# K's split projection: two accumulating matmuls of 128 columns in place of one of 256 and an addition

## The chip, the cores and the metric

The kernel runs on one core of a Trainium2 chip. Its engines, by the names of the profile, are PE (TensorE: matmuls; PEld are its weight loads), DVE (VectorE), ACT (ScalarE), POOL (GpSimd) and SP (SyncE, which issues nearly all DMAs). The metric is the device time of one execution in microseconds (us), lower is better.

## The reference

Linear attention with a feature map, followed by a block that mixes tokens and channels. What matters here is the first half; `phi(k)` begins with the product that the change rewrites.

```python
# q, k, v: (8, 8, 576, 64) float32; w_phi: (64, 128)
def phi(x):
    proj = np.einsum('bhsd,df->bhsf', x, w_phi)
    proj = proj - np.max(np.abs(proj), axis=-1, keepdims=True)
    return np.concatenate([np.exp(proj), np.exp(-proj)], axis=-1)
q_p, k_p = (phi(q), phi(k))
kv = np.einsum('bhsf,bhsd->bhfd', k_p, v)
z = np.sum(k_p, axis=2)
num = np.einsum('bhsf,bhfd->bhsd', q_p, kv)
den = np.einsum('bhsf,bhf->bhs', q_p, z)[..., None] + 1e-06
x = num / den            # heads joined: (8, 576, 512)
# then, per batch, with U (576 x 32), V (32 x 576), w_ch1 (512 x 2048), w_ch2 (2048 x 512):
h = x.transpose(0, 2, 1) @ U @ V
u = x + h.transpose(0, 2, 1)
out = u + np.maximum(u @ w_ch1, 0.0) @ w_ch2
```

## The kernel before

**Pairs of heads.** Attention works on pairs of heads of one batch, 8 x 4 = 32 pairs (`Pair`). Of the 576 tokens of a head, 512 are the main part, in four tiles of 128; the last 64 are the tail. For each pair the steps are: projecting K's tail and head 0 (`s_project_k0`), head 1 and Q's tail (`s_project_k1`), Q (`s_project_q0`, and the second half in `s_kv0_q1`), the sums over tokens of features times V (`kv_main`, line 448), and Q's features times these sums (`out_main`, line 487). The steps of one pair are interleaved with the output steps of the pair before.

**Split values.** Float32 products on TensorE are made here from parts in the type fp32r: a value is its rounded part (hi) plus what is left (lo). Batches 0 and 1 project K with plain float32 matmuls (line 389). Batches 2 to 7, with 24 pairs and thus 48 calls of `project_k_split`, use the parts. There `T[0]` holds K turned around, 128 partitions with the 64 hi parts and the 64 lo parts of a column one above the other, as [128, 2, 512]: the second index is the half of the tokens, the last is head and token within the half. `w_hl` is [128, 2, 128]: w_phi's hi part and its lo part, each written twice, one above the other. A matmul of a block of 128 tokens of `T[0]` (the weights) with `w_hl[:, n, :]` therefore gives (k_hi + k_lo) times one part of w_phi; the sum over n = 0, 1 is the projection.

**The call before the change** (lines 396 to 410). For each s of 0, 1, one PSUM bank `pk` takes two matmuls of 256 columns (line 404): each multiplies a block of tokens with both parts at once, and leaves the two products side by side. ACT copies the half that belongs to w_lo into the not yet used first half of the feature tile `kp` (line 407), and DVE adds the half that belongs to w_hi, into the second half of `kp` (line 408). Then `k_features` follows: the largest absolute value of each token (DVE, line 353), its subtraction (DVE, line 355), and the two exponentials (ACT, lines 358 and 359). In batches 0 and 1 `k_features` reads the PSUM bank directly.

**The tails** are the other place where parts of w_phi accumulate: `project_k_tail` (lines 378 and 379) and `project_q_tail` (lines 416 and 417) issue two matmuls of 128 columns of fp32r into the same columns of a bank.

**PSUM.** Eight banks in three groups: "at" with 3 banks (all tiles of attention: transposed tails `tT`, `pkt`, `pk`, `pqt`, `pq`, `kv_ps`, `xpt`, `xp`, and some of the token mixing), "ph" with 1 (hidden units of the mixer) and "o" with 4 (the mixer's outputs). A tile of a group waits until the tile that had its bank before is no longer read.

**The channel mixer** is most of TensorE's work: `hidden` (line 631) and `add` (line 652), each three matmuls of 512 columns for one product, one chunk of 128 hidden units after the other. `Pace` deals out the chunks of a batch among the attention steps of the next one, so TensorE finds matmuls while a step of attention waits for ACT and DVE.

**Order.** The program is built with `schedule_with_timeline_sim=True`: the framework's planner lays down each engine's order from its own estimated costs when the kernel is built; on the chip each engine runs its instructions in that order, and TensorE takes its matmuls in order.

Of the kernel before, what the change touches and what calls it, by code (L numbers as in the profile page):

```python
# [17 lines left out]
ALU = mybir.AluOpType  # L18
# [3 lines left out]
P = 128  # L22
# [3 lines left out]
def tile_kernel(  # L26
# [12 lines left out]
    nc = tc.nc  # L39
    B, H, S, D = q.shape  # L40
    F = w_phi.shape[1]
# [6 lines left out]
    NT = S // P  # L48
# [38 lines left out]
    w_hl = const.tile([P, 2, F], F32R, name="w_hl")  # L87
# [166 lines left out]
    class Pair:  # L254
# [140 lines left out]

        def project_k_split(self, g):

            kp = self.k_tile(g, NT)
            k_w = kp[:, :, F:2 * F]
            for s in range(2):  # L400
                pk = self.ps(f"pk{g}{s}_").rearrange("p (t n f) -> p t n f", t=2, n=2)
                for i in range(2):
                    cs = slice((2 * g + s) * P, (2 * g + s + 1) * P)
                    nc.tensor.matmul(  # L404
                        pk[:, i, :, :], self.T[0][:, i, cs], w_hl, start=True, stop=True)
                ts_ = slice(s, NT, 2)
                nc.scalar.copy(out=kp[:, ts_, 0:F], in_=pk[:, :, 1, :])
                nc.vector.tensor_tensor(
                    out=k_w[:, ts_, :], in0=pk[:, :, 0, :], in1=kp[:, ts_, 0:F], op=ALU.add)
            return self.k_features(g, k_w, kp)  # L410

        def project_q_tail(self):
            pq = self.ps("pqt")
# [535 lines left out]
```

## Time and profile before

| | us |
|---|---|
| median of two runs | 1218.74 (1218.65 to 1218.82) |
| the profiled execution | 1219.22 |
| its span, first to last instruction | 1217.4 |
| matmuls of line 404, x192: sum by the profile | 35.0 |
| copies of line 407 on ACT, x96 | 33.3 |
| additions of line 408 on DVE, x96 | 37.5 |
| first and last start of a matmul on line 404 | 197.0 and 977.8 |

Busy times of PE are sums over matmuls that overlap, with modelled ends, so the distance from one start to the next is what a matmul costs in a row of matmuls. Groups of instructions are written as line, engine, operation, out<-in, partitions x elements and count, then busy time in us and the mean of one in ns, then the idle time of the engine before them and what ended it. In the order of time a row gives the start, the length, the engine and the count of instructions merged into it.

### The profile page before, as it was taken

The page shows a single profiled execution, that of the slowest core. Times are in us where ns is not written, and L with a number is a line of the kernel's source. Part 1 is how long each engine was busy: PE and PEld are TensorE (multiplying, and loading weights), DVE is VectorE, ACT ScalarE, POOL GpSimd, SP SyncE. Part 2 cuts the span into 40 slices and gives each one's busy share as a digit, 9 for nine tenths or more (in the row PEclk, how much of TensorE's full clock was granted, in tenths as well). Part 3 has the DMA queues.
Part 4 walks back from the last instruction along what each step waited for, and adds up shares of the span by engine and source line. Part 5 has one row for each costly group of instructions (what it writes and reads, how often), then busy time and mean ns, then how long its engine had stood idle before and what let it go on. Part 6 is the DMA issues. An engine that isn't in the chain of part 4 may idle for free.

```text
span 1217.4 us, 18242 instructions
## 1 busy us (share of the span) xinstructions
PE 1193.5 (98%) x6669; PEld 1029.9 (85%) x6669; DVE 667.5 (55%) x1482; ACT 537.2 (44%) x1151; POOL 204.9 (17%) x154
## 2 busy tenths in 40 slices
PE   6999998999999999999999999999999999999998
PEld 5977887888888888888888888888888888888886
DVE  5667678765566556764647556765656542311211
ACT  5778787454443545344435454344444431111110
POOL 3334444211110111011111111011101110000000
PEclk8999999999999999999999999999999999999999
DMA  4686121331235123431244123521343015410201
GB/s 115 218 273 238 48 62 30 104 99 30 65 95 111 42 48 87 87 99 30 66 121 108 29 54 85 130 49 29 93 102 99 1 53 145 119 35 1 69 1 35
DMA packets 248290, 100.61 MB, mean 83 GB/s; under 512 B 215304, under 2 KB 227848, under 8 KB 248200
## 3 DMA queue, kind: packets, MB, share of 16 engines
q1 hardware_dynamic: 246928, 98.16, 30.9%
q10 hardware_dynamic: 1272, 1.28, 0.4%
q8 instruction: 53, 0.87, 0.3%
q14 instruction: 37, 0.30, 0.1%
HBM read 78.41 MB, written 20.97 MB: 82 GB/s over the span
## 4 chain that ended last, share of the span: by engine, by line
PE 88%; DVE 5%; DMA 2%; ACT 2%; SPq 1%; issue 1%; POOL 0%; DVEq 0%; ACTq 0%; POOLq 0%
PE ph L631 31%; PE o L652 30%; PE kv_ps L448 8%; PE xp L487 8%; PE pk L404 2%; PE pp L567 1%; PE kv_ps L441 1%; PE xpt L474 1%; PE pq L427 1%; PE pq L428 1%; SPq L270 1%; PE pq L432 1%; DVE w L240 1%; PE vp L585 1%; PE pk L389 1%
## 5 line engine op out<-in xcount | busy, mean ns | idle before, releaser
L631 PE MATMUL ph<-uT_hi,w 128*128 128x512 f32 x1152 | 389.3, 395 | 1.7 <-ACT uT_hi L248 1.1
L652 PE MATMUL o<-w,h_hi 128*128 128x512 f32 x1152 | 327.7, 395 | 0.7 <-ACT h_hi L636 0.7
L631 PEld LDWEIGHTS ph<-uT_hi,w 128*128 128x128 f32 x1152 | 216.3, 188 | 46.8 <-ACT uT_hi L248 1.8
L652 PEld LDWEIGHTS o<-w,h_hi 128*128 128x128 f32 x1152 | 211.1, 188 | 41.9 <-ACT h_hi L636 1.4
L631 PE MATMUL ph<-uT_lo,w 128*128 128x512 f32 x576 | 225.0, 391 | 0.3 <-DVE uT_lo L249 0.3
L636 ACT ACTIVATE h_hi<-ph 128x512 fp32r<-128x512 f32 x144 | 86.0, 597 | 278.9 <-PE ph L631 268.0
L637 DVE SCALAR_TENSOR_TENSOR h_lo<-ph,h_hi 128x512 fp32r<-128x512 f32 x144 | 98.7, 685 | 176.7 <-ACT h_hi L636 175.4
L652 PE MATMUL o<-w,h_lo 128*128 128x512 f32 x576 | 192.2, 395 | 0.0
L368 POOL PARTITION_ALL_REDUCE qp<-qp x64 | 127.0, 1984 | 296.8 <-ACT qp L367 274.8
L487 PEld LDWEIGHTS xp<-kv,qp 128*128 128x128 f32 x1024 | 122.6, 192 | 5.4 <-ACT w L239 0.8
L448 PEld LDWEIGHTS kv_ps<-vb,kp 128*128 128x128 f32 x1024 | 124.3, 192 | 2.8
L631 PEld LDWEIGHTS ph<-uT_lo,w 128*128 128x128 f32 x576 | 108.3, 188 | 21.6 <-DVE uT_lo L249 0.8
L487 PE MATMUL xp<-kv,qp 128*128 128x65 f32 x1024 | 122.9, 272 | 1.1 <-DVE x L466 0.7
L448 PE MATMUL kv_ps<-vb,kp 128*128 128x65 f32 x1024 | 123.7, 270 | 0.0
L652 PEld LDWEIGHTS o<-w,h_lo 128*128 128x128 f32 x576 | 105.2, 188 | 20.5 <-DVE h_lo L637 0.2
L358 ACT ACTIVATE kp<-kp 128x512 f32<-128x512 f32 x64 | 40.4, 632 | 125.9 <-DVE kp L355 88.7
L368 POOL PARTITION_ALL_REDUCE qp_t<-qp_t x32 | 27.3, 853 | 401.1 <-ACT qp_t L367 401.1
L324 DVE TENSOR_TENSOR T<-raw,T 64x512 fp32r<-64x512 f32 x96 | 68.2, 711 | 34.0 <-ACT T L323 31.5
L323 ACT CAST T<-raw 64x512 fp32r<-64x512 f32 x96 | 59.4, 618 | 34.7 <-PE pq L428 26.0
L320 DVE STREAM_TRANSPOSE raw<-raw 128x512 f32<-128x512 f32 x48 | 34.1, 711 | 67.8 <-DMA raw<-in_q_dram 24.8
L370 ACT ACTIVATE qp<-qp 128x512 f32<-128x512 f32 x64 | 40.4, 632 | 50.6 <-DVE qp L369 50.1
L145 POOL INT64_ADD w_ab<-w_ab x32 | 44.9, 1404 | 67.8 <-DVE w_ab L141 63.0
(125 smaller groups left out, 1324.2 us busy)
## 6 DMA issues: line engine op xcount, KB each, us to landing
words<-in_moe_w_ch_dram SPq DMA_DIRECT2D x32, 512.0 KB, 8.4
w<-kept SPq DMA_DIRECT2D x30, 512.0 KB, 4.0
vb<-in_v_dram SPq DMA_DIRECT2D x64, 128.0 KB, 2.4
u_dram<-x SPq DMA_DIRECT2D x32, 256.0 KB, 2.1
st<-u_dram SPq DMA_DIRECT2D x16, 512.0 KB, 3.8
out_dram<-st SPq DMA_DIRECT2D x32, 256.0 KB, 2.3
y<-u_dram SPq DMA_DIRECT2D x112, 64.0 KB, 2.2
raw<-in_k_dram SPq DMA_DIRECT2D x192, 32.0 KB, 1.8
```

The source lines that it names most:

```text
L145: nc.gpsimd.int64_add(a64, a64, b64)
L323: nc.scalar.copy(out=m[here, s, :], in_=x_[here])
L324: nc.vector.tensor_sub(m[there, s, :], x_[here], f32(m[here, s, :]))
L358: nc.scalar.activation(out=kp[:, :, 0:F], in_=kp[:, :, F:2 * F], func=AF.Exp)
L368: nc.gpsimd.partition_all_reduce(qp[:, 0, :], qp[:, 1, :], P, ReduceOp.absmax)
L370: nc.scalar.activation(out=qp[:, 0, :], in_=qp[:, 1, :], func=AF.Exp)
L448: nc.tensor.matmul(self.kv_v[:, f, g, :], kp[:, t, f * F:(f + 1) * F], self.vb[:, g, t, :], start=False, stop=(t == NT - 1), skip_group_ch ...
L487: nc.tensor.matmul(xv[:, c, :], qp[:, f, c * P:(c + 1) * P], self.kv[:, f, c // 2 if self.split else s, :], start=(f == 0), stop=(f == 1))
L631: nc.tensor.matmul(ph, w1_part(f, l, c), r[:, c, :], start=(n == 0), stop=(n == 3 * NCC - 1))
L636: on_act = nc.scalar.activation(out=h_hi, in_=ph, func=AF.Relu)
L637: on_dve = nc.vector.scalar_tensor_tensor(out=h_lo, in0=ph, scalar=0.0, in1=f32(h_hi), op0=ALU.max, op1=ALU.subtract)
L652: ins = nc.tensor.matmul(self.o[t], l[:, cs], w2_t[f][:, r, :], start=(f == 0 and n == 0), stop=(f == NFC - 1 and n == 2))
```

## The change

The projection of one head now takes one bank, four blocks of 128 columns, one for each tile of 128 tokens. For each tile two matmuls with the same weights follow one another: the first with w_hi, the second with w_lo, accumulating into the same 128 columns. The copy on ACT and the addition on DVE are gone; `k_features` gets the bank itself and reads it in lines 353 and 355, as in batches 0 and 1. The feature tile is no longer a place for the lo product.

```diff
         def project_k_split(self, g):
 
-            kp = self.k_tile(g, NT)
-            k_w = kp[:, :, F:2 * F]
-            for s in range(2):
-                pk = self.ps(f"pk{g}{s}_").rearrange("p (t n f) -> p t n f", t=2, n=2)
-                for i in range(2):
-                    cs = slice((2 * g + s) * P, (2 * g + s + 1) * P)
+            pk = self.ps(f"pk{g}_").rearrange("p (t f) -> p t f", f=F)
+            for t in range(NT):
+                lhs = self.T[0][:, t // 2, (2 * g + t % 2) * P:(2 * g + t % 2 + 1) * P]
+                for n in range(2):
                     nc.tensor.matmul(
-                        pk[:, i, :, :], self.T[0][:, i, cs], w_hl, start=True, stop=True)
-                ts_ = slice(s, NT, 2)
-                nc.scalar.copy(out=kp[:, ts_, 0:F], in_=pk[:, :, 1, :])
-                nc.vector.tensor_tensor(
-                    out=k_w[:, ts_, :], in0=pk[:, :, 0, :], in1=kp[:, ts_, 0:F], op=ALU.add)
-            return self.k_features(g, k_w, kp)
+                        pk[:, t, :], lhs, w_hl[:, n, :], start=(n == 0), stop=(n == 1))
+            return self.k_features(g, pk, self.k_tile(g, NT))
```

## The prediction

> **What bounds the kernel now.** I read the profile in this order: the page's busy times and its chain, then the busy times by stage, then the groups of the lines that the change touches, then the waits of TensorE, and last the order in time around single matmuls, because the price of a short matmul can be read nowhere else.
>
> ```profile
> span 1217.4 us, 18242 instructions
> PE 1193.5 (98%) x6669; PEld 1029.9 (85%) x6669; DVE 667.5 (55%) x1482; ACT 537.2 (44%) x1151; POOL 204.9 (17%) x154
> PEclk8999999999999999999999999999999999999999
> PE 88%; DVE 5%; DMA 2%; ACT 2%; SPq 1%; issue 1%; POOL 0%; DVEq 0%; ACTq 0%; POOLq 0%
> ```
>
> TensorE is busy for 98% of the span, the granted clock is full after the first slice, and 88% of the chain that ended last are matmuls. There are as many weight loads as matmuls: 6669 of each, so every matmul brings a load of its own.
>
> ```profile
> 0.00:197.00 197.00, 179.80 (x1115) 155.98 (x1116) 130.85 (x302) 145.45 (x299) 83.33 (x77) 0.97 0.49 150
> 197.00:985.00 788.00, 786.50 (x4520) 685.53 (x4520) 481.86 (x1087) 359.17 (x795) 119.65 (x76) 1.00 0.30 72
> 985.00:1217.40 232.40, 227.22 (x1038) 188.44 (x1037) 54.82 (x94) 32.60 (x59) 1.94 (x1) 1.00 0.21 60
> ```
>
> These are three stretches: batches 0 and 1, then batches 2 to 7 with the split projection, then the end. The columns after the length are the busy times of PE, PEld, DVE, ACT and POOL. In the middle stretch, where all the edited code runs, PE is busy for 786.5 of 788.0 us; DVE has 306 us free and ACT 429 us. So only what TensorE has to do counts there: work taken from DVE and ACT is work beside the path, and a matmul added is time added.
>
> **The change, part by part.** These are the groups that it touches, and two forms that it will use:
>
> ```profile
> L408 DVE TENSOR_TENSOR kp<-pk,kp 128x256 f32<-128x256 f32 x96 | 37.5, 409 | 2.0 <-ACT kp L407 2.0
> L404 PE MATMUL pk<-w_hl,T 128*128 128x256 f32 x192 | 35.0, 286 | 0.0
> L407 ACT COPY kp<-pk 128x256 f32<-128x256 f32 x96 | 33.3, 371 | 32.1 <-PE pk L404 31.8
> L355 DVE TENSOR_TENSOR kp<-kp,mk 128x512 f32<-128x512 f32 x48 | 33.1, 690 | 1.2
> L353 DVE TENSOR_REDUCE mk<-kp 128x4 f32<-128x512 f32 x48 | 32.7, 681 | 1.2
> L355 DVE TENSOR_TENSOR kp<-pk,mk 128x512 f32<-128x512 f32 x16 | 11.0, 686 | 0.3
> L353 DVE TENSOR_REDUCE mk<-pk 128x4 f32<-128x512 f32 x16 | 10.9, 683 | 0.9 <-PE pk L389 0.9
> L379 PE MATMUL pkt<-w_hl,tail_T 128*128 128x128 f32 x24 | 6.6, 276 | 0.0
> ```
>
> *How often.* L407 and L408 run 96 times, twice in each of 48 calls; L404 runs 192 times, four in a call. Afterwards a call has eight matmuls of 128 columns: 384 in all, 192 more, each with a load of 128 columns of weights.
>
> *What leaves ACT and DVE.* 33.3 us of copies (L407) and 37.5 us of additions (L408). PE's 786.5 us cover both. The maximum and the subtraction (L353, L355) then read the bank itself, as the unsplit batches do already: 683 and 686 ns there against 681 and 690 ns from `kp`, so nothing changes. I take 0 for this part. The most that it can give back is PE's idle time of the stretch, 788.0 - 786.5 = 1.5 us.
>
> *What TensorE pays.* The mean duration of a matmul is no price, since matmuls overlap; the price is the distance from one start to the next. Matmuls in order of time around two calls:
>
> ```profile
> 210.00 0.39 PE L652 MATMUL o<-w,h_lo 128*128 128x512 f32 x1
> 210.23 0.40 PE L404 MATMUL pk<-w_hl,T 128*128 128x256 f32 x2
> 210.46 0.63 PE L652 MATMUL o<-w,h_hi 128*128 128x512 f32 x2
> ...
> 603.06 0.64 PE L404 MATMUL pk<-w_hl,T 128*128 128x256 f32 x4
> 603.53 0.62 PE L652 MATMUL o<-w,h_lo 128*128 128x512 f32 x2
> ```
>
> Two matmuls of 256 columns take from 210.23 to 210.46, 115 ns each. Four in a row take from 603.06 to 603.53, 118 ns each. I take 118 ns, as the longer sample, and so 472 ns for a call.
>
> For 128 columns the nearest rows are the two accumulating matmuls of the tails (L416 and L417, or L378 and L379): the same type, the same 128 columns, and for K's tail even the same weights twice and the same moving `w_hi`, `w_lo`.
>
> ```profile
> 211.16 0.63 PE L652 MATMUL o<-w,h_hi 128*128 128x512 f32 x2
> 211.62 0.22 PE L416 MATMUL pqt<-tail_T,w_hl 128*128 128x128 f32 x1
> 211.68 0.28 PE L417 MATMUL pqt<-tail_T,w_hl 128*128 128x128 f32 x1
> 211.79 0.45 PE L652 MATMUL o<-w,h_lo 128*128 128x512 f32 x1
> 212.08 0.62 PE L652 MATMUL o<-w,h_hi 128*128 128x512 f32 x2
> ```
>
> The second starts 0.06 us after the first, so 128 columns stream in 0.06 us, and accumulating in the same place costs no wait. But the pair isn't over with 0.12 us. Two L652 take from 211.16 to 211.62, 0.23 each. From 211.62 to 212.08 two short matmuls and one L652 take 0.46: the pair costs 0.23 us, 115 ns each, as much as a pair of 256 columns. The weight loads of the same moments show why:
>
> ```profile
> 211.63 0.19 PEld L417 LDWEIGHTS pqt<-tail_T,w_hl 128*128 128x128 f32 x1
> 211.73 0.19 PEld L652 LDWEIGHTS o<-w,h_lo 128*128 128x128 f32 x1
> 211.84 0.42 PEld L652 LDWEIGHTS o<-w,h_hi 128*128 128x128 f32 x2
> ...
> 203.57 1.86 PEld L487 LDWEIGHTS xp<-kv,qp 128*128 128x128 f32 x16 [0.57 <-DVE kp L408]
> ```
>
> Loads don't start closer than 0.10 to 0.11 us. Where matmuls are shorter than that, the loads set the step: the sixteen loads of L487, for matmuls of 65 columns, take 1.86 us, that is (1.86 - 0.19) / 15 = 111 ns each. A matmul of 256 columns just hides the next load behind its own streaming; one of 128 columns hides half of it. So for eight short matmuls in a row I take 112 ns each, near the long run: 896 ns a call.
>
> The Trainium skill, "TensorE: Matmul & The Clock Gate", section "LDWEIGHTS (loading the stationary operand)", gives a load's time as its columns over 1.2 GHz, an estimate of 107 ns for 128; this speaks against the change, and the trace agrees with its 111 ns. By 107 ns, and the gap of 109 ns that the same page's formula gives for 256 columns, the change would cost 48 x (8 x 107 - 4 x 109) = 20 us.
>
> *The sum.* 48 x (896 - 472) ns = +20.4 us on TensorE, and 0 for ACT and DVE. The profiled span becomes 1217.4 + 20.4 = 1237.8 us. That execution took 1219.2 us, 1.8 more than its span, and the median of the runs is 1218.74: on that, 1239.1 us, 1.7% more. The ends: the least is 48 x (8 x 111 - 4 x 118) = 20.0 us, less the 1.5 us of idle time, so 1237.2; the most is 48 x (8 x 115 - 4 x 115) = 22.1 us, so 1240.8. The planner will also place instructions anew; TensorE's waits that could come or go by it are the second rival's.
>
> *Nothing queues.* No DMA is added, removed or moved past another on SP or POOL, and no instruction but these. On PE the first of the eight waits for `T[0]` and a free bank, as the first of four did; behind it wait the next chunks of the mixer. The call takes one bank instead of two in turn; it is held until L355 ends and not until L408.
>
> **The rivals.** *First: the loads are hidden or left out, and the time stays.* For it speaks the 0.06 us from L416 to L417, and that both matmuls of a new group use the same weights. Eight would take 8 x 60 = 480 ns instead of 472, and the time would be 1218.74 + 48 x 0.008 = 1219.1. Against it: 6669 loads for 6669 matmuls, L379's among them with L378's weights, and the 0.11 us that follows each L417. The gap of N / 2.4 + 2.5 ns in the Trainium skill's same page, section "Back-to-back issue gap", would make this rival true, with an estimate of 48 x (8 x 55.8 - 4 x 109.2) ns = 0.5 us more; the trace bears it out only for the first step of a pair.
>
> *Between the two: only every second matmul waits for a load.* By the steps of 0.06 and 0.11 a pair costs 0.17, a call 680 ns, and the time is 1218.74 + 48 x 0.208 = 1228.7. Against it: that 0.17 leaves out the L652 after the pair, which keeps the array for 0.29 instead of 0.23. The same section states 81 ns a matmul for a stream of loads and matmuls of 128 columns; by that it would be an estimate of 1218.74 + 48 x (8 x 81 - 472) ns = 1227.2. No row here shows so short a step in a row.
>
> *Second, slower by over 2%: TensorE waits for the bank that L353 and L355 now hold.* The "at" group has three banks; `kv_ps` keeps one of them over several steps. The new bank is full only after 0.9 us, and then DVE reads it for 0.68 + 0.69 us, with whatever is queued before that. The next user of the bank (`pkt`, `xpt`, `xp`, `pq`) is behind it, and PE takes its matmuls in order. One such wait is there already:
>
> ```profile
> PEld xp L487 <- DVE kp L408: 0.6, 1, 0.6
> ```
>
> If each of the 48 calls caused a wait like it, that would be 29 us more: 1268. It takes only (1243.1 - 1239.1) / 48 = 0.08 us a call to pass 2%. Against it: the old code took two banks a call, each until its L408, and waited so once in 48 calls; and DVE loses 37.5 us of work that stood ahead of L353.
>
> *Third: the shorter chain for `kp` pays.* No row shows PE waiting for a feature of K in this stretch beyond single waits; with all 1.5 us it gives 1237.6, inside the forecast.
>
> **How the numbers follow.** Forecast with its ends: 0.77, with the third rival in it. Loads free: 0.04. Half of them: 0.05. Bank waits: 0.14. The predicted time is 1239.1. Its own range is 1237.2 to 1240.8. For 8 in 10 I reach down to 1235.0, since a plan laid anew can win back a wait of the first stretch, where PE is idle for 17 us, and up to 1246.0, into half of the bank waits; that leaves out about 0.04 + 0.05 + 0.07. A measurement of this kernel can tell about 2% from no change: that is 1194.4 and 1243.1. Slower by more: the bank waits and a little of the forecast's tail, 0.16. Faster by more: no row gives room for it, 0.01. Within: 0.83.
>
> **What would show it.** In the changed kernel's profile: 6861 matmuls and as many loads; no group on L407 and L408, ACT 33 and DVE 37 us less; the eight loads of a call 0.11 us apart, and about 0.90 us from its first start to the next matmul; the stretch of the split batches about 20 us longer with PE as busy as before. Wrong: steps of 0.06 us throughout, or fewer loads than matmuls (first rival); a group of waits of PE or PEld on DVE mk or kp L353 or L355 with several us in all (second rival). A difference of several us in the first 197 us would mean that the plan moved, and not the edited work.

## The result, and the profile after

The changed kernel takes 1246.85 us (two runs, 1245.56 and 1248.13), against 1218.74 before: a ratio of 1.0225, with a 95% interval of 1.0207 to 1.0242. It is slower by 28.1 us, where 20.4 were forecast. That is 6.05 us above the forecast's own range, which ended at 1240.8, and 0.85 us above the 1246.0 at which the range for 8 in 10 ended. A second set of four runs on another chip gave 1246.54 beside 1219.49 for the kernel before, a ratio of 1.0219 (1.0202 to 1.0236).

The page of the changed kernel. Its profiled execution is the slower of the two, 1248.13 us.

```profile
span 1246.3 us, 18451 instructions
PE 1220.8 (98%) x6859; PEld 1055.7 (85%) x6861; DVE 641.3 (51%) x1386; ACT 517.7 (42%) x1055; POOL 204.1 (16%) x154
PEclk9999998999999999999999999999999999999999
```

There are 6861 loads, as forecast (two records of matmuls are missing), 96 instructions fewer on DVE and on ACT, and still 98% of the span on PE. New is an 8 in the clock's row, in the slice from 187 to 218 us; the 8 in the first slice of the kernel before is gone.

The groups of the changed kernel, by line, with shapes kept apart. Behind the edit, line numbers are six smaller than in the kernel before: L631 there is L625 here, and L652 is L646.

```profile
L402 PE MATMUL pk<-w_hl,T 128*128 128x128 f32 x384 | 51.8, 274 | 0.4 <-DVE uT_lo L249 0.4
L402 PEld LDWEIGHTS pk<-w_hl,T 128*128 128x128 f32 x384 | 50.7, 194 | 3.4 <-DVE uT_lo L249 0.8
L355 DVE TENSOR_TENSOR kp<-pk,mk 128x512 f32<-128x512 f32 x64 | 43.5, 680 | 1.0
L353 DVE TENSOR_REDUCE mk<-pk 128x4 f32<-128x512 f32 x64 | 43.5, 679 | 2.3 <-PE pk L389 0.9 <-PE pk L402 0.9
```

L353 and L355 take 679 and 680 ns on the bank: about the same as from `kp` before (681 and 690). The price of the new matmuls shows in the order of time, first PE's rows around a call, then PEld's.

```profile
277.81 1.09 PE L402 MATMUL pk<-w_hl,T 128*128 128x128 f32 x8
278.74 0.27 PE L410 MATMUL pqt<-tail_T,w_hl 128*128 128x128 f32 x1
```

```profile
277.79 0.97 PEld L402 LDWEIGHTS pk<-w_hl,T 128*128 128x128 f32 x8
```

Eight matmuls take 278.74 - 277.81 = 0.93 us, and their loads stand (0.97 - 0.19) / 7 = 0.111 us apart. 0.90 and 0.11 were forecast. So the matmuls cost about what was said, and about 8 us came from something else. Two views show it: the waits of TensorE's weight loads from 196 us on, before the change and after it, and the busy times of three stretches after it (length, then PE, PEld, DVE, ACT, POOL, then the granted clock).

```profile
PEld pkt L378 <- issue: 3.1, 1, 3.1
PEld ph L631 <- DVE den_t L461: 1.0, 1, 1.0
PEld ph L631 <- ACT uT_hi L248: 0.6, 1, 0.6
PEld ph L631 <- DVE uT_lo L249: 0.6, 1, 0.6
...
PEld pkt L378 <- DVE xt L586: 0.5, 1, 0.5
PEld o L652 <- DVE h_lo L637: 0.2, 1, 0.2
```

```profile
PEld pkt L378 <- issue: 3.5, 1, 3.5
PEld ph L625 <- DVE h_lo L631: 2.1, 3, 1.1
PEld vp L579 <- DVE x L580: 1.1, 1, 1.1
PEld tT L310 <- ACT qp L367: 1.1, 1, 1.1
PEld pk L402 <- DVE uT_lo L249: 0.8, 1, 0.8
PEld kv_ps L435 <- DVE x L460: 0.4, 1, 0.4
PEld pt L597 <- DVE x L580: 0.4, 1, 0.4
PEld pt L597 <- DVE st L667: 0.2, 1, 0.2
```

```profile
197.00:985.00 788.00, 784.03 (x4543) 685.21 (x4544) 446.08 (x966) 330.80 (x681) 114.21 (x73) 0.99 0.31 72
...
545.00:548.40 3.40, 3.40 (x10) 2.61 (x9) 1.00 (x4) 1.77 (x4) 0.00 (x0) 0.51 0.80 207
197.00:203.70 6.70, 6.54 (x22) 5.81 (x23) 5.67 (x12) 4.09 (x8) 2.81 (x2) 0.50 0.33 60
```

The waits add up to 9.6 us after, and to 6.6 before (the row shown here in the prediction, 0.6 for L408, among them): 3.0 more. None of the new ones names L353 or L355. `h_lo`, `vp` and `pt` belong to the mixer and the token mixing, `tT` and `kv_ps` to attention; only `pk` L402 is an edited line, and it waits for L249 of the token mixing. Nor did L353 or L355 hold up DVE ahead of the longest wait for `h_lo`: DVE itself stood idle there until ACT was done.

```profile
543.89 0.69 DVE L631 SCALAR_TENSOR_TENSOR h_lo<-ph,h_hi 128x512 fp32r<-128x512 f32 x1 [1.12 <-ACT h_hi L630]
```

At 956 us it is the same, and only ahead of the shortest of the three, 0.2 us at 414.9, does L353 run right before `h_lo`.

And for 6.7 + 3.4 us the granted clock was half, with PE busy: an estimate of 5.0 us lost, half of that time. Together 20.4 + 3.0 + 5.0 = 28.4, against 1246.3 - 1217.4 = 28.9 us of span. The kernel before has half the clock as well, for 10.2 us at its beginning (from 7.7 us on), but this leaves no mark on the difference: the first matmul of the split batches starts at 196.8 us there and at 197.2 us after the change.

### The profile page after: what moved, and what is told of

It reads as the page before. It is cut to its first block, busy times and chain, and to the rows that moved or that the text cites. A ratio compares the mean times of both kernels' runs of the same rounds, so it can differ in the third digit from the quotient of the medians.

```text
span 1246.3 us, 18451 instructions
## 1 busy us (share of the span) xinstructions
PE 1220.8 (98%) x6859; PEld 1055.7 (85%) x6861; DVE 641.3 (51%) x1386; ACT 517.7 (42%) x1055; POOL 204.1 (16%) x154
## 4 chain that ended last, share of the span: by engine, by line
PE 86%; DVE 5%; DMA 4%; ACT 2%; SPq 2%; issue 1%; POOL 1%; DVEq 0%; ACTq 0%
PE ph L625 29%; PE o L646 29%; PE xp L481 8%; PE kv_ps L442 8%; PE pk L402 3%; PE pp L561 1%; PE xpt L468 1%; PE kv_ps L435 1%; DVE T L324 1%; PE pk L389 1%; PE pq L421 1%; PE pq L426 1%; SPq L270 1%; DMA raw<-in_k_dram 1%; PE pq L422 1%
## 5 line engine op out<-in xcount | busy, mean ns | idle before, releaser
L625 PE MATMUL ph<-uT_hi,w 128*128 128x512 f32 x1152 | 386.8, 398 | 2.5 <-DVE h_lo L631 1.7
L646 PE MATMUL o<-w,h_hi 128*128 128x512 f32 x1152 | 347.7, 397 | 0.7 <-ACT h_hi L630 0.7
L625 PEld LDWEIGHTS ph<-uT_hi,w 128*128 128x128 f32 x1152 | 217.8, 189 | 48.5 <-DVE h_lo L631 2.7
L646 PEld LDWEIGHTS o<-w,h_hi 128*128 128x128 f32 x1152 | 210.6, 188 | 42.6 <-ACT h_hi L630 1.4
L625 PE MATMUL ph<-uT_lo,w 128*128 128x512 f32 x576 | 226.6, 393 | 0.0
L646 PE MATMUL o<-w,h_lo 128*128 128x512 f32 x576 | 208.5, 393 | 0.0
L631 DVE SCALAR_TENSOR_TENSOR h_lo<-ph,h_hi 128x512 fp32r<-128x512 f32 x144 | 98.6, 685 | 191.2 <-ACT h_hi L630 191.0
L625 PEld LDWEIGHTS ph<-uT_lo,w 128*128 128x128 f32 x576 | 109.2, 190 | 21.1 <-DVE uT_lo L249 0.2
L646 PEld LDWEIGHTS o<-w,h_lo 128*128 128x128 f32 x576 | 107.4, 188 | 21.7
L324 DVE TENSOR_TENSOR T<-raw,T 64x512 fp32r<-64x512 f32 x96 | 72.4, 754 | 28.0 <-ACT T L323 25.5
```

What stands on the lines that cost most here:

```text
L324: nc.vector.tensor_sub(m[there, s, :], x_[here], f32(m[here, s, :]))
L625: nc.tensor.matmul(ph, w1_part(f, l, c), r[:, c, :], start=(n == 0), stop=(n == 3 * NCC - 1))
L631: on_dve = nc.vector.scalar_tensor_tensor(out=h_lo, in0=ph, scalar=0.0, in1=f32(h_hi), op0=ALU.max, op1=ALU.subtract)
L646: ins = nc.tensor.matmul(self.o[t], l[:, cs], w2_t[f][:, r, :], start=(f == 0 and n == 0), stop=(f == NFC - 1 and n == 2))
```

## The experiments

Three theories stood at first, named in the expectations: ORDER, PRICE and BANK. All kernels ran beside the kernel before on the same chip; differences are to its median there.

**The changed kernel once more** (`again`), no edit.

> The changed kernel once more, for its spread. Three theories of the 28 us. ORDER: the 192 added matmuls cost about 20 us by their weight loads, and the other 8 are waits of TensorE that a new plan of the order brings (the mixer's next chunk behind DVE's h_lo, for the one ph bank), with a time at a lower clock after some of them; these need not fall alike in every run, so runs between 1243 and 1248. BANK: the 8 us are waits for the bank that lines 353 and 355 now hold. PRICE: there are no such waits to speak of, and a short matmul costs 132 ns instead of 112: (28.1 / 48 + 0.472) / 8 us. BANK and PRICE: the same in every run, 1246 to 1248.

Measured 1246.54 us, from 1246.29 to 1247.39: +27.1. The range of the runs doesn't tell the theories apart. The profile of this set has one stretch at half the clock, not two:

```profile
196.10:202.90 6.80, 6.35 (x22) 5.71 (x23) 5.76 (x12) 4.37 (x9) 2.82 (x2) 0.50 0.33 59
```

**The matmuls alone** (`e1_split_keep`).

```diff
-                    nc.tensor.matmul(
-                        pk[:, i, :, :], self.T[0][:, i, cs], w_hl, start=True, stop=True)
+                    for n in range(2):
+                        nc.tensor.matmul(
+                            pk[:, i, n, :], self.T[0][:, i, cs], w_hl[:, n, :],
+                            start=True, stop=True)
```

> The matmuls alone: eight of 128 columns a call, each into a place of its own, with the two banks, the copies on ACT and the additions on DVE as before. ORDER: the 20 us of loads, and waits according to this plan's own order: 1239 to 1247. BANK: the banks are read and released as before, so 1239, within 1 us. PRICE: all 28 us, 1247. If loads were hidden: 1219.

Measured 1249.31 us, +29.8 (ratio 1.0241, 1.0226 to 1.0257). BANK isn't needed for an excess: the banks are read and let go as before, and the excess over 20 us is larger still. The result lies above what ORDER allowed, too, so the theory was left with PRICE beside it.

**The bank alone** (`e2_half`), from the changed kernel.

```diff
-                for n in range(2):
-                    nc.tensor.matmul(
-                        pk[:, t, :], lhs, w_hl[:, n, :], start=(n == 0), stop=(n == 1))
+                nc.tensor.matmul(pk[:, t, :], lhs, w_hi, start=True, stop=True)
```

> The other part alone: one bank read by lines 353 and 355, and only the first of each two matmuls (w_hi), four of 128 columns a call; K's product with w_lo is left out. ORDER: four loads a call as before, 4 x 112 instead of 472 ns, so 1217.5, and up to 4 more by the order: 1217 to 1222. BANK: the bank is held as in the changed kernel, so 1217.5 + 8 = 1225. PRICE: 4 x 132 instead of 472 ns, 1221.4.

Measured 1222.74 us, +3.3 (ratio 1.0029, 1.0020 to 1.0039). With four loads a call nearly all of the loss is gone. It is above ORDER's 1222 by a little and above PRICE's 1221.4, so it decides nothing between them. It is below BANK's 1225, though three of the ten runs took 1225. Its profile again has a stretch at half the clock, worth 1.7 us:

```profile
196.90:200.30 3.40, 3.40 (x11) 2.84 (x11) 3.03 (x8) 1.70 (x4) 2.12 (x2) 0.51 0.46 85
```

**Two banks for `ph`, two for `at`** (`e4_banks`), from the changed kernel.

```diff
-    BANKS = {"at": 3, "ph": 1, "o": 4}
+    BANKS = {"at": 2, "ph": 2, "o": 4}
```

> The changed kernel with two banks for ph and two for at, instead of one and three; computes the same. ORDER: a chunk of the mixer no longer waits for the h_lo of the one before, so most of the 8 us go: 1239 to 1242, unless two banks for attention bring waits of their own. BANK: with fewer banks the held one is waited for more often: 1255 or more. PRICE: no change, 1247.

Measured 1341.59 us, +122. All theories missed. With two banks attention starves, the token mixing first:

```profile
PEld vp L579 <- DVE x L580: 13.1, 15, 1.3
PEld ph L625 <- DVE uT_lo L249: 7.8, 10, 1.5
```

The wait for `h_lo` isn't in the top rows any more, but so much else is late that this says nothing of the 8 us.

**The old order for the new work** (`e5_old_order`). The planner's order of the kernel before was read from its built program and written out, one list for each engine, with each matmul of 256 columns replaced by the two that do its work, and the copies and additions struck out. The lists enter as edges that fix the order of issue and add no wait:

```diff
+    for engine, code in ORDER.items():
...
+        for a, b in zip(at, at[1:]):
+            tc.add_manual_dep(
+                seq[b], seq[a].name, mybir.DependencyInfo(
+                    mybir.DependencyClass.NoSync, mybir.DependencyReason.DATA),
+                reason="lay_down")
```

> The changed kernel's work in the order of the kernel before: every engine's order is written out by hand as the planner had it there, with two matmuls of 128 columns in the place of each one of 256, and without the copies and additions. Computes the same. ORDER: the 192 added loads stay, +20.4 us, and the waits of TensorE fall back to those of the kernel before: 1239 to 1241. PRICE (all 28 us are the price of the short matmuls) or BANK (the bank that lines 353 and 355 hold): 1246 or more.

Measured 1243.35 us, +23.9 (ratio 1.0186, 1.0169 to 1.0203): less than the changed kernel, but 2.4 us above ORDER's upper end. PE's rows of the place where the rest went:

```profile
247.44 0.61 PE L597 MATMUL pt<-ident,x 128*128 128x128 f32 x4
250.13 0.63 PE L402 MATMUL pk<-w_hl,T 128*128 128x128 f32 x4 [2.09 <-DVE kp L355]
250.60 0.45 PE L625 MATMUL ph<-uT_hi,w 128*128 128x512 f32 x1
```

This is the second rival of the prediction, once: a call waits 2.1 us until L355 has let go of the bank of the call before. In the old order DVE has other work between. The clock then halves for 3.4 us, from 251.6 on, an estimate of another 1.7: 1219.44 + 20.4 + 2.1 + 1.7 = 1243.6. The sum is rough. It leaves out that the kernel before had 3.5 us of other waits behind the first one, of which `e5_old_order` has 0.3, and that the split batches start 1.7 us later in this profile, at 198.5 us. For the changed kernel's own work, the old order saved 27.1 - 23.9 = 3.2 us.

**The new order for the old work** (`e6_new_order`), in the same way the other way round; copies and additions were left to the planner.

> The converse: the work of the kernel before, four matmuls of 256 columns a call with copies and additions, in the order that the planner laid down for the changed kernel. Computes the same. ORDER: the waits come with the order, without one more matmul: 1222 to 1227. PRICE or BANK: no change, 1219 to 1220.

Measured 1270.54 us, +51 (1.0417, 1.0385 to 1.0449). An order alone can cost that much without one matmul more, but the size was missed by far: PE waits most for a bank that L408 still reads, and the order that was taken over was made for a kernel without L408.

```profile
PEld xp L487 <- DVE kp L408: 15.3, 11, 1.9
PEld ph L631 <- DVE h_lo L637: 5.3, 8, 1.9
```

**Sixteen matmuls of 64 columns** (`e7_cols64`), from the changed kernel: the same columns, twice the loads.

```diff
+                for h in range(2):
+                    cs = slice(h * F // 2, (h + 1) * F // 2)
                     for n in range(2):
                         nc.tensor.matmul(
-                        pk[:, t, :], lhs, w_hl[:, n, :], start=(n == 0), stop=(n == 1))
+                            pk[:, t, cs], lhs, w_hl[:, n, cs], start=(n == 0), stop=(n == 1))
```

> The suspected price doubled: the changed kernel with sixteen matmuls of 64 columns a call instead of eight of 128, the same columns streamed in all, 384 more weight loads. Computes the same. If the load sets the step: 48 x 8 x 0.112 = 43 us more than the changed kernel, 1289, give or take 5 for its own waits. If columns set it: 1247. If half of the loads were hidden: 1268.

Measured 1287.63 us: 68.2 more than the kernel before on its chip, where the changed kernel had 27.1 more, so 41.1 us for 384 loads, or 107 ns each. This quotient is no exact price, since it holds the kernel's own waits and clock, but it is near the 43 us of "the load sets the step" and far from the 0 of "columns set it".

**Pinned matmuls** (`e8_pinned`), from the changed kernel: `tc.keep_in_program_order` around each of L402's matmuls.

> The changed kernel with each matmul of the split projection pinned behind the matmul traced before it. The planner's order then differs from the changed kernel's in one stretch only, batch 2's second half (about 230 to 265 us in the profile), where the changed kernel has some 3 us of waits: at the token mixing (vp), at the transposed tail (tT) and at pk. ORDER: these waits go or change and nothing else does: 1243 to 1247. PRICE or BANK: 1246.5, within 0.5.

Measured 1246.35 us, +26.9. No verdict: the waits at `vp`, `tT` and `pk` were all still there, so nothing was taken away.

**The matmuls alone, in the old order** (`e9_split_old_order`): e1's edit with the lists of the kernel before, nothing struck out.

> The work of e1_split_keep (the kernel before with two matmuls of 128 columns in the place of each one of 256, copies and additions kept) in the order of the kernel before, on every engine. e1 took 1249.3 in the planner's own order. If a short matmul costs 112 ns and the rest of e1's 30 us came with its order: 1219.4 + 20.4 = 1239.8, within 1.5. If the price is more than that and the order adds little: 1246 or more.

Measured 1239.64 us, +19.5 (ratio 1.0160, 1.0146 to 1.0174). This settles it for e1's work, which is the same instruction for instruction: e1 had +29.8, so about 10 us of e1's loss is order. Here are the waits of PEld from 196 us on, the longest of e1 first, then all of e9, and e9's stretch of the split batches. The wait at `pkt` is in e9 too, but ends before 196 us. (L633 and L654 of both are L631 and L652 of the kernel before.)

```profile
PEld o L654 <- ACT h_hi L638: 3.2, 3, 1.7
PEld pkt L378 <- issue: 2.9, 1, 2.9
PEld kv_ps L443 <- PE tT L310: 2.3, 5, 0.5
PEld pt L605 <- DVE x L588: 1.6, 1, 1.6
```

```profile
PEld ph L633 <- DVE uT_lo L249: 0.5, 1, 0.5
PEld ph L633 <- ACT uT_hi L248: 0.4, 1, 0.4
```

```profile
197.00:985.00 788.00, 787.50 (x4593) 689.28 (x4594) 475.53 (x1062) 353.99 (x775) 115.65 (x74) 1.00 0.31 72
196.00:199.40 3.40, 3.40 (x12) 2.88 (x11) 2.98 (x8) 2.77 (x7) 1.02 (x1) 0.50 0.42 67
```

PE is busy for 787.5 of 788 us, so nearly all that is left of the loss is the added loads. The second row shows that this profile, too, has 3.4 us at half the clock, an estimate of 1.7 us; against that it has 0.9 us of waits where the kernel before has 3.5 behind the first one. PRICE, with 28 us for the loads, falls.

**Filling the idle 3 us ahead of the split batches** (`e10_fill_after`, `e11_fill_before`, `e12_fill_bank`). Each has twelve matmuls more, into a `ph` bank, or (the last) into `pkt`. `e10_fill_after` and `e12_fill_bank` are the changed kernel and `e11_fill_before` is the kernel before, each with its own order written out as above. The edit of `e12_fill_bank`:

```diff
             kT = self.tail_T[:, 0, :]
+            if (self.b, self.h0) == (SPLIT, 0):
+                for _ in range(12):
+                    nc.tensor.matmul(pk, w_hi, v_all[:, 0:SM], start=True, stop=True)
```

> The changed kernel in its own order, with twelve matmuls of 512 columns (their results are not used) laid into TensorE's idle 3 us before the first matmul of the split batches. In the changed kernel's profiles a stretch of 6.8 us at half the clock follows on that idle time. If the idle time sets it off: the stretch goes, 3.4 us less, 1243.1. If not: 1246.5.

> The same twelve matmuls in the kernel before, in its own order. Its profile shows full clock after the same idle time. If half the clock after it is the changed kernel's alone: no change, 1219.4. If it falls on some runs of the kernel before as well: about 1 us less and the runs closer together.

> As e10_fill_after, but the twelve matmuls go into the bank of the first split tail, pkt, before its own two matmuls, so that they wait for nothing of DVE: e10's waited for DVE's h_lo and so left the idle time as it was. If the idle time sets off the 6.8 us at half the clock: they are gone from the profile, PE's idle time before L379 is under 1 us, and the time is 1243.1. If the clock falls without the idle time as well: 1246.5.

The first two missed: 1249.69 us (+29.6) and 1223.65 (+3.6). The added matmuls themselves waited for the bank until DVE's `h_lo`, 4.1 and 4.4 us, and then ran at half the clock. e12 filled the gap: PE is busy for all of 193 to 197 us at full clock. Yet it took 1249.21 us, +28.1, no less than the changed kernel. PE came to the second call's bank sooner and waited there, and the clock halved after that wait:

```profile
203.05 0.72 PE L649 MATMUL o<-w,h_hi 128*128 128x512 f32 x2
205.13 1.08 PE L405 MATMUL pk<-w_hl,T 128*128 128x128 f32 x8 [1.36 <-DVE den_t L459]
```

```profile
206.60:210.00 3.40, 3.40 (x11) 2.73 (x10) 3.11 (x9) 3.35 (x7) 1.28 (x1) 0.51 0.02 5
193.00:197.00 4.00, 4.00 (x23) 3.18 (x21) 3.85 (x6) 3.98 (x8) 1.44 (x1) 1.00 0.11 18
```

So the half clock went with the idle time and came back behind the next wait, where some of the time won was given back. `e8_pinned`, whose profile keeps the full clock at 194 us, has the same wait of 1.4 us at 203.8 us and 3.4 us at half the clock behind it. More can't be said of the 1249.21: the profiled run is the fastest of the five, 1246.41.

## Why the prediction was wrong

- *TensorE pays 20.4 us:* right. 0.111 us from load to load, 0.93 us for a call, e9 with 19.5 us (17.8 to 21.2 by its interval), and e7, where doubling the loads costs another 41.1.
- *ACT and DVE give back nothing:* right in direction; ACT is 20 us and DVE 26 us less busy in the profile, with no gain to be seen. (33 and 37 were forecast. The page counts time in which two instructions of an engine overlap once, so not all of a group's time goes with it.)
- *First rival, loads hidden, and the case between, every second one:* false. As many loads as matmuls, each 0.11 us apart, although both matmuls of a group use the same weights.
- *Second rival, the bank held by L355:* the mechanism exists (2.1 us, once, in e5), but the changed kernel's own waits don't name it, and e1 loses as much without it. Its bound was right, though: 4 us from anywhere were enough to pass 2%. "Slower by more" had a chance of 0.16, nearly all of it for this rival, so it came for another reason than the one that was given.
- *The failed step* is the sentence that the planner will place instructions anew, with its price. I put it at nothing in the sum, and at most at the idle time that could be won back, and gave waits that come only to the second rival and its bank. The planner's order for the changed work has 3.0 us more of waits, at `h_lo`, `vp`, `tT` and `pk`, and in the profiled execution 5.0 us at half the clock. The prediction took the granted clock as full behind the first slice, as the page of before shows it, and has no term for it. Its sign of a moved plan, a difference in the first 197 us, looked at the wrong place: that stretch is only 0.4 us longer, and the waits moved inside the split batches.

The sum of the parts closes to about 0.5 us for one execution. That the order makes e1's loss larger is shown by runs, e1 against e9; for the changed kernel the old order took away 3.2 us, and the rest of its 7 to 8 us is read from the trace. Why the planner's order is worse here was not tried: its estimates for a short matmul may differ from 0.11 us, but no run tests that. Nor was a run made that has the changed kernel's work, the old order and no wait for the bank; 1239.6, that is 1243.35 - 2.1 - 1.7, is an estimate for it.

## What to carry to other kernels

Where TensorE is the bound, count weight loads, not columns: in these runs a matmul of this type cost its load, about 0.11 us, with 64 columns and with 128, and hardly more with 256 (115 to 118 ns). So halving the width from 256 doubled the price of the same product, and the work taken from ACT and DVE did not pay for it. Where a planner lays down the order, an edit in one place moves waits in others; give that a term of its own, a few us here, and separate it from the work by running the new work in the old order.

## What the runs showed of the hardware

The granted clock fell to one half for 3.4 us at a time, or for a multiple of that: 6.8 us in the changed kernel, 10.2 us at the beginning of the kernel before. From 190 us to the last matmul, and leaving out `e4_banks` and `e6_new_order` with their many waits, each fall came during an idle time of TensorE of half a microsecond or more, or at most 1.6 us behind one. But no length of idle time decides it. The clock fell with idle times of 3.1 us and 1.0 us (the changed kernel, at 194 and 543.7 us), 2.65 us (e9, at 193 us) and 1.4 us (e12, at 203.8 us); it stayed full with 2.7 us in the kernel before and 3.3 us in e5, at the same place, and with 1.8 us in e12, at 235.6 us. The Trainium skill, "TensorE: Matmul & The Clock Gate", section "Part 1: The HAM clock gate", has the clock fall to half after an idle window of about 3.4 us that runs free of the kernel. The lengths of the stretches agree with it; all these idle times are shorter than such a window, and there the measurement decides.

What 3.4 us at half the clock cost can be read where `again` has full clock and the changed kernel has not. These are the same two matmuls, on both sides of that stretch, first in the changed kernel, then in `again`:

```profile
544.98 0.56 PE L625 MATMUL ph<-uT_lo,w 128*128 128x512 f32 x1
554.31 0.48 PE L625 MATMUL ph<-uT_hi,w 128*128 128x512 f32 x1
...
544.40 0.40 PE L625 MATMUL ph<-uT_lo,w 128*128 128x512 f32 x1
552.16 0.48 PE L625 MATMUL ph<-uT_hi,w 128*128 128x512 f32 x1
```

The distance is 9.33 us in one and 7.76 in the other, so 1.6 us were lost, near the estimate of 1.7. Whether such stretches make up the 1 to 3 us by which single runs of one kernel differ is not shown.
